# In a fused attention and mixture-of-experts kernel, the third expert's row gathers are tied behind the second expert's last low half

## The chip, the cores and the metric

The kernel runs on one core of one Trainium2 chip. The metric is device microseconds of one execution of the whole program. The kernel before took 590.61 us (median of three runs, 588.82 to 591.28). The profiled execution, from which all rows below come, took 590.45 us; its span, from the first profiled instruction to the last, is 588.60 us, so 1.85 us lie around the span.

The five engines are called as the profile calls them: PE (matmuls), DVE (VectorE), ACT (ScalarE), POOL (GpSimd) and SP (SyncE, which only issues DMAs here). Each engine runs its own queue of instructions strictly in order; semaphores tie the queues together.

## The reference

```
kv  = einsum('bhsd,bhse->bhde', k, v)            # 8 x 8 heads, 576 rows, 64 wide
out = einsum('bhsd,bhde->bhse', q, kv)
x   = out / sqrt(mean(out*out) + 1e-6) * g_norm  # then 4608 rows of 512
logits = x @ w_gate                              # 8 experts, the best one is taken
e = argmax(logits); gate = softmax(logits)[e]
h = relu(x[rows of e] @ w1[e])                   # 512 -> 1024
y = h @ w2[e]                                    # 1024 -> 512
out[row] = gate * y                              # at most 1152 rows per expert
```

## The kernel before

**Stages.** The first half of the program computes the attention, normalises and routes the rows, and writes each row (with its scale and its gate) to the DRAM table `x_dram`. The second half takes the eight experts in order of their row counts, r = 0 to 7, with fixed row budgets of 704, 672, 640, 624, 592, 576, 560 and 512. The expert r = 0 is begun early; "the second expert" is r = 1 (672 rows), "the third expert" is r = 2 (640 rows).

**An expert's matmuls.** Inputs and weights are split into a high and a low fp16 half, and three products stand for one fp32 product. The first layer makes eight blocks (j = 0 to 7) of hidden units: 24 matmuls (line 522) into a PSUM bank `hp`, of which there are two in turn; ACT then writes the high half `hh` (line 527) and DVE the low half `hl` (line 530), which frees the bank. The second layer (lines 568 and 577) multiplies by `w2`, ACT scales the result (`ysb`, line 593), and POOL scatters it to the output (line 598).

**An expert's rows.** While expert r is multiplied, `rows_beside(r + 1)` brings the rows of the next one, in tiles of 128 (r = 1: five full tiles and one of 32; r = 2: five). Each tile is gathered by an indirect DMA that POOL issues (`fetch`, line 433, into `xg`, four buffers), normalised into `xm` (line 441, two buffers; on DVE or POOL for r = 1, on POOL otherwise), its gate is copied (line 446, POOL), ACT rounds it to the high half (`pair`, line 465, two buffers), POOL subtracts for the low half (line 469), and SP issues a transposing DMA into `xs` (line 473). The first layer's products for all columns wait for these transposes.

**An expert's weights.** `weights(r + 1)` loads `raw` in eight pieces through SP (line 321), and DVE takes the largest magnitude of each eighth (`am`, line 337). Two tiny matmuls (lines 350 and 357) spread the maximum over the partitions, DVE works out a scale, ACT writes high halves (`w1h`, `w2h`, line 371), DVE low halves (`w1l`, `w2l`, line 377).

**What sets the order.** Every step is registered with `op(engine and planned duration, function, dependencies, key, ...)`, and `Plan.place()` plays the whole program through with the planned durations: an engine that is free takes, of the operations that are ready, the one with the smallest key. Instructions are emitted in the order found, so each engine's queue is fixed before the program runs. In `rows_beside` the gathers have the key of their expert's turn and everything behind them `key + 1`, so a ready gather of the third expert goes ahead of work of the same rank on POOL, and it is issued as soon as an `xg` buffer is planned to be free.

Of the kernel before, what the change touches and what calls it, by code (L numbers as in the profile page):

```python
# [78 lines left out]
class Ring:  # L79
# [3 lines left out]
    def new(self):  # L83
        self.holds.append(Hold(self.holds[-self.n] if len(self.holds) >= self.n else None))
        return self.holds[-1]
# [8 lines left out]
class Plan:  # L94
# [5 lines left out]
    def op(self, ways, fn, deps=(), key=0.0, takes=(), uses=(), late=0.0):  # L100

        ways = [ways] if isinstance(ways[0], str) else list(ways)
        o = Op(ways, fn, [d for d in deps if d is not None], list(takes), key, late)
        for h in takes + uses if isinstance(takes, tuple) and isinstance(uses, tuple) else list(takes) + list(uses):
            h.users.append(o)
        self.ops.append(o)
        return o
# [56 lines left out]
def attention_moe_kernel(  # L164
# [17 lines left out]
    P = 128  # L182
# [96 lines left out]
    first = cst.tile([P, E], F32, name="first")  # L279
# [130 lines left out]
    def spans(s0, s1):  # L410

        cuts = [s0] + list(range((s0 // P + 1) * P, s1, P)) + [s1]
        return [(a, b - a, NHI if a % P else a // P) for a, b in zip(cuts, cuts[1:])]
# [212 lines left out]
    def slots(pool, reg_ap, s0=0):  # L626

        c_reg = nc.vector.value_load(reg_ap, min_val=0, max_val=(E - 1) * NHI)
        both = []
        for tab_, nm in ((gidx_tab, "gi"), (sidx_tab, "si")):  # L630
            t = pool.tile([P, NHI + 1], I32, name=f"{nm}{s0}", bufs=3)
            nc.vector.tensor_copy(t[:, 0:NHI], tab_[:, ds(c_reg, NHI)])  # L632
            if s0 % P:
                nc.vector.tensor_copy(t[0:P - s0 % P, NHI:NHI + 1], t[s0 % P:P, s0 // P:s0 // P + 1])
            both.append(t)
        return both
# [27 lines left out]
    op = plan.op  # L664
# [411 lines left out]
    early = {}  # L1076
# [414 lines left out]
    op = plan.op  # L1491
# [59 lines left out]
    def rows_beside(r, key):  # L1551

        hold, sl, st = new("xs"), new("slots"), {}

        def cut(e):
            st["gi"], st["si"] = slots(mo, perm_i[0:1, 1, r:r + 1])

        cut_ = op(("V", 0.4), cut, [early["rank"]], key, (sl,))
        n = len(spans(0, BUDGET[r]))
        gates, turned, first, sent, asked = [], [], None, [], []  # L1560
        for i in range(n):
            xg, xm, pair = new("xg"), new("xm"), new("pair")

            def fetch(e, i=i):
                if i == 0:
                    st["x"] = Rows(mo, st["gi"], 0, BUDGET[r], BM, 4)
                st["x"].fetch(i)

            o = op(("P", 1.05), fetch, [cut_, first], key, (hold, xg), (sl,))
            first = first or o  # L1570
            asked.append(o)
            o = op(("D", GATHER), None, [o], key, (), (xg,))
            a = op([("V", 0.61), ("P", NORM)] if r == 1 else ("P", NORM),
                   lambda e, i=i: st["x"].norm(i, nc.vector if e == "V" else nc.gpsimd), [o], key - 5 if r == 1 else key + 1,
                   (xm,), (xg,))
            gates.append(op(("P", 0.25), lambda e, i=i: st["x"].gate(i, nc.gpsimd), [a], key + 1, (), (xg, hold)))
            a = op(("A", 0.52), lambda e, i=i: st["x"].pair_high(i), [a], key + 1, (pair,), (xm, hold))
            a = op(("P", PAIR), lambda e, i=i: st["x"].pair_low(i), [a], key + 1, (), (xm, pair, hold))
            a = op(("S", TURN), lambda e, i=i: st["x"].pair_turn(i), [a], key + 1, (), (pair, hold))
            sent.append(a)  # L1580
            turned.append(op(("D", TURNED), None, [a], key + 1, (), (pair, hold)))
        return st, hold, sl, gates, turned, sent, asked
# [50 lines left out]
    o = op(("S", 0.01), moved, [early["scaled"]], -9 * KEY, (), tuple(ews))  # L1633
# [6 lines left out]
    for r in range(E):  # L1640
        products(r, *args)
        key = KEY * r
        if r + 1 < E:
            before = [] if r > 1 else sent
            st, xs_hold, sl, gates, turned, sent, asked = rows_beside(r + 1, key + ROWS)
            sets, zs, w_holds = weights(r + 1, key + 1, before, asked[4:4 + 1] if r == 0 else [])
            args = (lambda st=st: st["x"], turned, turned, gates, xs_hold, lambda st=st: st["si"], sl, sets, zs, w_holds, 0,
                    BUDGET[r + 1])
        else:
            steps, o = plan_rest(), early["later"]  # L1650
            for _ in range(68):
                o = op(("V", 0.2), lambda e: next(steps, None), [o], key + 1)
# [36 lines left out]
```

## Time and profile before

| | |
|---|---|
| median of three runs | 590.61 us (588.82 to 591.28) |
| profiled execution | 590.45 us, span 588.60 us |
| PE busy | 535.5 us, 91% of the span |
| DVE, ACT, POOL busy | 381.2, 256.5, 222.5 us |
| mean granted PE clock | 0.976 of full speed |

PE is the engine that is busy longest. Of its idle time in the second half, the stretch of interest here is around 220 us from the span's start, where the matmuls of the second expert begin; those of the third begin at 287 us. Busy shares are read per stretch, since the stages have different limits, and a duration of POOL in the profile includes time in which the instruction was held up.

### The profile page before, as it was taken

How to read it: one execution, taken by the hardware profiler on the slowest of the kernel's cores; microseconds unless marked ns; L12 is line 12 of the kernel's file. 1: busy time of each engine (PE TensorE's matmuls, PEld its weight loads, DVE VectorE, ACT ScalarE, POOL GpSimd, SP SyncE). 2: the span in 40 equal slices, each digit the busy share in tenths (PEclk: the TensorE clock that was granted, in tenths of full speed). 3: DMA queues.
4: the chain of work that ended last, by engine and by line, in shares of the span. 5: the costliest groups of instructions: out<-in, count | busy, mean ns of one | idle time of the engine just before them, and what ended most of it. 6: DMA issues, size and time to landing. Idle time of an engine off the chain costs nothing.

```text
span 588.6 us, 11591 instructions
## 1 busy us (share of the span) xinstructions
PE 535.5 (91%) x4339; PEld 359.2 (61%) x4339; DVE 381.2 (65%) x999; ACT 256.5 (44%) x498; POOL 222.5 (38%) x299
## 2 busy tenths in 40 slices
PE   1888899878987997999999999999999999999995
PEld 1887798778533654654665467467648747845442
DVE  2376688889995877999998556719637634740200
ACT  1456476769621355382825151543525255211210
POOL 6002043355315677466541724364163452011011
PEclk9999799988999997999999999999999999999998
DMA  7999999957228768688861753646266332001001
GB/s 200 265 273 327 331 298 363 334 186 252 91 91 293 213 145 288 150 268 221 244 215 56 209 167 120 195 112 220 73 174 190 117 73 76 1 30 45 1 19 48
DMA packets 94302, 102.56 MB, mean 174 GB/s; under 512 B 51314, under 2 KB 75890, under 8 KB 93216
## 3 DMA queue, kind: packets, MB, share of 16 engines
q1 hardware_dynamic: 86240, 70.43, 44.2%
q0 software_dynamic: 8000, 31.32, 15.1%
q8 instruction: 36, 0.59, 0.4%
q14 instruction: 26, 0.21, 0.1%
HBM read 73.13 MB, written 20.61 MB: 159 GB/s over the span
## 4 chain that ended last, share of the span: by engine, by line
PE 38%; DVE 21%; issue 18%; DMA 11%; POOL 5%; ACT 3%; SPq 3%; POOLq 0%; DVEq 0%; ACTq 0%
PE hp L522 14%; PE yp L568 14%; DMA out_dram<-ysb,si 6%; DVE am L337 4%; DMA q_sb<-in_q_dram 4%; DVE w2l L377 4%; PE op L789 3%; DVE w1l L377 2%; PE yp L577 2%; PE qp L771 2%; DVE hl L530 2%; DVE ss L818 1%; SPq L686 1%; SPq L685 1%; PE a L707 1%
## 5 line engine op out<-in xcount | busy, mean ns | idle before, releaser
L522 PE MATMUL hp<-xs,w1h 128*128 128x320 f16 (+6 forms) x896 | 135.1, 302 | 5.9 <-DMA xs<-pair 4.3
L522 PEld LDWEIGHTS <-w1h 128*128 128x128 f16 x960 | 93.7, 99 | 47.4 <-issue 9.2
L598 POOL DMA_INDIRECT out_dram<-ysb,si x41 | 43.9, 1071 | 138.0 <-ACT ysb L593 103.2
L568 PEld LDWEIGHTS <-hh 128*128 128x128 f16 x560 | 54.3, 98 | 64.5 <-issue 1.9
L527 ACT ACTIVATE hh<-hp 128x320 f16<-128x320 f32 (+7 forms) x64 | 40.8, 638 | 116.1 <-PE hp L522 113.2
L337 DVE TENSOR_REDUCE am<-raw 128x1 f32<-128x512 f32 x120 | 75.6, 674 | 5.7 <-DMA raw<-in_moe_w_dram 5.5
L522 PE MATMUL hp<-xs,w1l 128*128 128x320 f16 (+6 forms) x448 | 71.6, 300 | 0.0
L530 DVE SCALAR_TENSOR_TENSOR hl<-hp,hh 128x320 f16<-128x320 f32 (+7 forms) x64 | 47.2, 737 | 36.0 <-ACT hh L527 35.8
L469 POOL TENSOR_TENSOR pair<-xm,pair 128x512 f16<-128x512 f32 (+5 forms) x35 | 42.6, 1222 | 73.2 <-ACT pair L465 73.1
L568 PE MATMUL yp<-w2h,hl 128*128 128x512 f16 x272 | 66.1, 386 | 0.0
L568 PE MATMUL yp<-w2h,hh 128*128 128x512 f16 x272 | 64.4, 379 | 0.8 <-ACT ysb L593 0.8
L568 PE MATMUL yp<-w2l,hh 128*128 128x512 f16 x272 | 64.4, 379 | 0.0
L789 PE MATMUL op<-kv_bd,qt 128*128 128x144 f32 (+1 forms) x384 | 58.5, 295 | 6.0 <-ACT qt L672 2.4
L593 ACT ACTIVATE ysb<-yp,ysc 128x512 f32<-128x512 f32 (+5 forms) x40 | 27.4, 684 | 83.2 <-PE yp L568 69.5
L522 PEld LDWEIGHTS <-w1l 128*128 128x128 f16 x480 | 46.7, 98 | 19.1
L433 POOL DMA_INDIRECT xg<-x_dram,gi x41 | 43.8, 1067 | 36.6 <-DVE gi L632 24.2
L789 PEld LDWEIGHTS op<-kv_bd,qt 128*128 128x128 f32 x384 | 50.7, 197 | 9.7 <-ACT o_sb L672 3.2
L377 DVE SCALAR_TENSOR_TENSOR w2l<-raw,sw,w2h 128x512 f16<-128x512 f32 x64 | 49.2, 815 | 9.7 <-ACT w2h L371 9.7
L377 DVE SCALAR_TENSOR_TENSOR w1l<-raw,sg,w1h 128x512 f16<-128x512 f32 x64 | 47.3, 788 | 0.9 <-ACT w1h L371 0.8
L568 PEld LDWEIGHTS <-hl 128*128 128x128 f16 x280 | 27.2, 99 | 33.5 <-issue 2.6
L371 ACT ACTIVATE w2h<-raw,sw 128x512 f16<-128x512 f32 x62 | 39.6, 711 | 5.9 <-PE yp L577 3.5
L371 ACT ACTIVATE w1h<-raw,sg 128x512 f16<-128x512 f32 x62 | 39.6, 711 | 4.8 <-DVE sg L366 3.8
(249 smaller groups left out, 666.3 us busy)
## 6 DMA issues: line engine op xcount, KB each, us to landing
raw<-in_moe_w_dram SPq DMA_DIRECT2D x64, 512.0 KB
x_dram<-o_sb POOLq DMA_DIRECT2D x8, 1152.0 KB
k_sb<-in_k_dram SPq DMA_DIRECT2D x16, 512.0 KB
v_sb<-in_v_dram SPq DMA_DIRECT2D x16, 512.0 KB
q_sb<-in_q_dram SPq DMA_DIRECT2D x16, 512.0 KB
x_dram<-o_sb POOLq DMA_DIRECT2D x8, 144.0 KB
k_sb<-in_k_dram SPq DMA_DIRECT2D x16, 64.0 KB
v_sb<-in_v_dram SPq DMA_DIRECT2D x16, 64.0 KB
```

Source lines behind the costliest of these rows:

```text
L337: nc.vector.tensor_reduce(out=am()[:, p:p + 1], in_=raw[:, sl(p)], axis=AX.X, op=ALU.max, apply_absolute_value=True)
L371: nc.scalar.activation(wh[:, sl(p)], raw[:, sl(p)], AF.Copy, scale=z["s"])
L377: nc.vector.scalar_tensor_tensor(out=wl[:, sl(p)], in0=raw[:, sl(p)], scalar=z["s"], in1=wh[:, sl(p)], op0=ALU.mult, op1=ALU.subtract)
L433: nc.gpsimd.indirect_dma_start(out=self.xg[i][0:n], out_offset=None, in_=x_dram[0:self.rows, :], in_offset=bass.IndirectOffsetOnAxis(ap=se ...
L469: nc.gpsimd.tensor_tensor(out=pair[0:n, 1], in0=self.xm[i][0:n], in1=pair[0:n, 0], op=ALU.subtract)
L522: nc.tensor.matmul(self.view(hp)[:, u], lhsT=w[:, c, j * P:(j + 1) * P], rhs=x[:, c, u * hw:(u + 1) * hw], start=(t == 0 and c == 0), stop ...
L527: nc.scalar.activation(self.out(self.hh, j), self.view(hp), AF.Relu)
L530: nc.vector.scalar_tensor_tensor(out=self.out(self.hl, j), in0=self.view(hp), scalar=0.0, in1=self.out(self.hh, j), op0=ALU.max, op1=ALU.s ...
L568: nc.tensor.matmul(yp[0:n, 0:DM], lhsT=h[:, j, o:o + n], rhs=w[:, j, :], start=(m == 0), stop=(m == len(self.terms) - 1))
L593: nc.scalar.activation(self.ysb[0:n], yp[0:n, 0:DM], AF.Copy, scale=self.ysc[0:n, i:i + 1])
L598: nc.gpsimd.indirect_dma_start(out=out[:, :], out_offset=bass.IndirectOffsetOnAxis(ap=self.sidx[0:n, col:col + 1], axis=0), in_=ysb[0:n], ...
L789: nc.tensor.matmul(ph.t[:, j * m:(j + 1) * m], lhsT=qt.t[:, i * P:(i + 1) * P], rhs=x, start=True, stop=True)
```

## The change

One dependency is added. For r = 1 each `pair_low` (line 469) is noted in `early["lows", 1]`; for r = 2 each gather depends, besides the slots and the expert's first gather, on the last of those. The list exists for r = 1 alone, so only the third expert's five gathers get the new dependency. No operation is added or taken away; the planner is run anew and may order all queues otherwise.

```diff
-            o = op(("P", 1.05), fetch, [cut_, first], key, (hold, xg), (sl,))
+            o = op(("P", 1.05), fetch, [cut_, first] + early.get(("lows", r - 1), [])[-1:], key, (hold, xg), (sl,))
...
             a = op(("P", PAIR), lambda e, i=i: st["x"].pair_low(i), [a], key + 1, (), (xm, pair, hold))
+            if r == 1:
+                early.setdefault(("lows", r), []).append(a)
```

POOL's queue in the kernel before, from the gates of the second expert's third and fourth tile to the scatter after its last low half. `gi_2751` are the row numbers of the third expert; `pair` of line 469 is a low half of the second:

```order
L446 COPY gt<-xg 128x1 x2
L433 DMA xg<-x_dram,gi_2751 128x576 x2
L469 TENSOR_TENSOR pair<-xm,pair 128x512 x2
L446 COPY gt<-xg 128x1
L433 DMA xg<-x_dram,gi_2751 128x576
L598 DMA out_dram<-ysb,si_2601 4608x512
L446 COPY gt<-xg 32x1
L433 DMA xg<-x_dram,gi_2751 128x576
L469 TENSOR_TENSOR pair<-xm,pair 128x512
L469 TENSOR_TENSOR pair<-xm,pair 32x512
L598 DMA out_dram<-ysb,si_2601 4608x512
```

The same stretch in the changed kernel:

```order
L446 COPY gt<-xg 128x1 x2
L469 TENSOR_TENSOR pair<-xm,pair 128x512
L441 TENSOR_TENSOR xm<-xg 128x512
L446 COPY gt<-xg 128x1
L469 TENSOR_TENSOR pair<-xm,pair 128x512
L598 DMA out_dram<-ysb,si_2601 4608x512
L469 TENSOR_TENSOR pair<-xm,pair 128x512
L446 COPY gt<-xg 32x1
L469 TENSOR_TENSOR pair<-xm,pair 32x512
L598 DMA out_dram<-ysb,si_2601 4608x512
L433 DMA xg<-x_dram,gi_2751 128x576 x3
```

Four gathers of the third expert have gone from between the low halves to behind them, and the normalisation of the second expert's fifth tile (line 441) has come over from DVE. One scatter (line 598) stays between the fourth and the fifth low half.

ACT's queue before, where the second expert's first layer begins:

```order
L593 ACTIVATE ysb<-yp,ysc 64x512
L371 ACTIVATE w2h_2648<-raw_2645,sw_3242 128x512 x8
L527 ACTIVATE hh<-hp 128x672
L465 CAST pair<-xm 128x512 x2
L527 ACTIVATE hh<-hp 128x672 x3
```

And in the changed kernel:

```order
L593 ACTIVATE ysb<-yp,ysc 64x512
L371 ACTIVATE w2h_2648<-raw_2645,sw_3246 128x512 x6
L527 ACTIVATE hh<-hp 128x672
L371 ACTIVATE w2h_2648<-raw_2645,sw_3246 128x512 x2
L465 CAST pair<-xm 128x512
L527 ACTIVATE hh<-hp 128x672
```

The first `hh` of the second expert stands behind six high halves of `w2` in place of eight. DVE's queue has the like: the first `hl` (line 530) came behind seven low halves of `w2` (line 377) and comes behind six.

## Rows read from the trace of the kernel before

**Rows 1.** What PE waited for, 200 to 300 us; columns in the first line.
```profile
engine line waited for: us in total, times, longest us
PE hp L522 <- DMA xs<-pair: 4.3, 1, 4.3
PE pt_max L357 <- DVE bm L354: 1.5, 2, 1.2
PE yp L588 <- DVE bmax L361: 1.2, 1, 1.2
PE hp L522 <- DVE p2t L302: 1.2, 1, 1.2
```

**Rows 2.** The same, 300 to 590 us.
```profile
PE hp L522 <- DVE hl L530: 0.4, 1, 0.4
```

**Rows 3.** Timeline of PE: start, duration, line, operation, tiles, count, [idle before it].
```profile
221.00 0.31 PE L522 MATMUL hp<-xs,w1h 128*128 128x336 f16 x1
225.65 4.16 PE L522 MATMUL hp<-xs,w1h 128*128 128x336 f16 x15 [4.34 <-DMA xs<-pair]
229.65 1.30 PE L522 MATMUL hp<-xs,w1l 128*128 128x336 f16 x8
230.79 2.44 PE L522 MATMUL hp<-xs,w1h 128*128 128x336 f16 x16
```

**Rows 4.** Stretches: length, busy per engine, granted PE clock, DMA share, GB/s.
```profile
219.00:222.00 3.00, 1.13 (x10) 0.75 (x7) 1.10 (x6) 0.74 (x2) 2.90 (x3) 1.00 0.46 150
222.00:225.00 3.00, 0.00 (x0) 0.00 (x0) 2.42 (x1) 3.00 (x6) 2.91 (x3) 0.61 1.00 199
225.00:229.00 4.00, 3.35 (x13) 1.79 (x14) 4.00 (x6) 1.83 (x3) 2.81 (x5) 0.50 0.77 265
```

**Rows 5.** SP's queue: the transpose of the second expert's last tile.
```profile
222.23 1.18 SPq L473 DMA_TRANSPOSE xs<-pair  x1
```

**Rows 6.** Timeline of POOL, 210 to 226 us.
```profile
210.47 1.52 POOL L469 TENSOR_TENSOR pair<-xm,pair 128x512 f16<-128x512 f32 x1 [2.42 <-ACT pair L465]
...
212.39 3.94 POOL L433 DMA_INDIRECT xg<-x_dram,gi  x1 [0.27 <-POOL gt L446]
216.64 1.51 POOL L598 DMA_INDIRECT out_dram<-ysb,si  x1 [0.31 <-DVE bm L354]
...
219.63 2.28 POOL L469 TENSOR_TENSOR pair<-xm,pair 128x512 f16<-128x512 f32 x2
222.08 1.02 POOL L598 DMA_INDIRECT out_dram<-ysb,si  x1 [0.17 <-ACT ysb L593]
223.12 2.10 POOL L441 TENSOR_TENSOR xm<-xg 128x512 f32<-128x512 f32 x2
```

**Rows 7.** Timeline of ACT, 211 to 232 us.
```profile
211.89 0.69 ACT L593 ACTIVATE ysb<-yp,ysc 128x512 f32<-128x512 f32 x1 [0.27 <-PE yp L568]
212.79 0.62 ACT L465 CAST pair<-xm 128x512 f16<-128x512 f32 x1 [0.21 <-DMA xs<-pair]
215.28 0.62 ACT L465 CAST pair<-xm 32x512 f16<-32x512 f32 x1 [1.87 <-DMA xs<-pair]
...
221.84 4.99 ACT L371 ACTIVATE w2h<-raw,sw 128x512 f16<-128x512 f32 x8
```

**Rows 8.** Timeline of DVE: two trains of weight lows, the first and last `hl`.
```profile
212.75 2.72 DVE L377 SCALAR_TENSOR_TENSOR w1l<-raw,sg,w1h 128x512 f16<-128x512 f32 x4
...
222.59 3.19 DVE L377 SCALAR_TENSOR_TENSOR w2l<-raw,sw,w2h 128x512 f16<-128x512 f32 x1 [1.35 <-ACT w2h L371]
...
231.75 0.86 DVE L530 SCALAR_TENSOR_TENSOR hl<-hp,hh 128x672 f16<-128x672 f32 x1 [2.01 <-ACT hh L527]
...
258.28 0.85 DVE L530 SCALAR_TENSOR_TENSOR hl<-hp,hh 128x672 f16<-128x672 f32 x1
```

**Rows 9.** Busy time again, in the second expert's layers (columns as in Rows 4).
```profile
240.00:260.00 20.00, 20.00 (x131) 12.55 (x130) 19.66 (x42) 11.58 (x19) 12.50 (x11) 1.00 0.63 160
```

**Rows 10.** The third expert's last transpose on SP and its first matmuls.
```profile
250.53 1.23 SPq L473 DMA_TRANSPOSE xs<-pair  x1
...
287.22 2.33 PE L522 MATMUL hp<-xs,w1h 128*128 128x320 f16 x16
```

## The prediction

> **What bounds the kernel now.** The waits of PE come first, since PE is the engine that is busy longest. Between 200 and 300 us one of them is 4.3 us: the first layer of the second expert waits for a transposed tile [rows 1]; behind 300 us PE waits for 0.4 us on any other engine's result [rows 2]. So whatever PE gains near 220 us should still be there at the end, unless a stretch before 300 us takes it back. PE's timeline shows the wait: one matmul at 221.00, ending at 221.31, the next at 225.65 [rows 3]. It also shows a second cost. Fifteen matmuls then take 4.00 us from start to start (229.65 less 225.65); eight take 1.14 us a little later (230.79 less 229.65), so fifteen should take 2.14, and 1.86 us are lost. The stretches say why: PE had done nothing from 221.3 on, and the granted clock, 1.00 up to 222, is 0.61 in the mean over the next 3 us and 0.50, the lower of its two levels (1.2 of 2.4 GHz), from 225 to 229 [rows 4].
>
> What PE waited for is the transpose of the sixth tile, which SP issued at 222.23 [rows 5]; from there to 225.65 are 3.42 us, a landing. It was issued late because POOL was late. POOL finished the fourth low half at 211.99. The casts for the fifth and sixth were done on ACT at 213.41 and 215.90 [rows 7], but these two low halves ran only from 219.63 to 221.91: between stand a gather for the third expert that took 3.94 us, a scatter of 1.51 and another gather [rows 6]. The 3.94 us are no work of POOL: DVE's train of four `w1l` ran from 212.75 to 215.47 [rows 8], and the gather came through 0.86 us behind it.
>
> **The change part by part.** Up to the fourth low half POOL gets one thing more, the fifth tile's normalisation, 1.05 us each by the pair of 2.10, and its gate; POOL was idle for 2.42 us before that low half [rows 6], so this costs nothing, and the xm buffer it needs is free when the third low half ends.
>
> From there, by the order of the changed queue: the scatter, the fifth low half, a gate, the sixth, a scatter, and only then gathers. The scatter's data are ready at 212.58 (211.89 and 0.69) [rows 7]. Its price has two ends. At the low end it takes 1.02 us, as the scatter at 222.08 [rows 6]: then the fifth low half can run from 213.6, the sixth behind its cast at 215.90, ending at about 217.1, the transpose goes out there and lands at 220.5. PE would not wait at all, and 4.34 us go. At the high end it fares as the gather at 212.39 did beside the same DVE train: done at 216.4. Then the fifth low half ends at 217.6 (1.14 each, half of 2.28), with the gate (some 0.2) the sixth at 218.9, and the transpose lands at 222.35. PE waits 1.04 us from 221.31, and 3.3 us go. I take the high end: it is the nearest row, the same place beside the same four instructions. The scatter could also be no help at all if the low halves are held again and again; that is the first rival.
>
> By the Trainium skill ("SBUF — State Buffer", section "Who interferes with whom"), a DVE instruction with two SBUF inputs holds up only POOL instructions that read SBUF; writing DMA descriptors needs the other, the write side, which the page marks as inferred. `w1l` has two SBUF inputs, so by that rule the scatter would not be held and the sum below would be 6.2 us, a time of 584.3. The gather of 3.94 us that ended just behind the train [rows 6, 8] speaks against the rule, so the row decides.
>
> The clock is the second term. Its bounds are 0 and the 1.86 us worked out above. In 219 to 222 PE was idle for 1.87 of 3.00 us and the clock was still 1.00 [rows 4]; it fell only in the next 3 us, in which PE did nothing. With matmuls from 222.35 on, little of that idle time is left, and I take the whole 1.86 us. But if the clock falls all the same, this term is nothing.
>
> The sum is 3.3 + 1.86 = 5.2 us. What the moved work hides behind: the five gathers start some 8 us to 16 us later than they did, and their rows are wanted at 287.22, while the last transpose of the third expert went out at 250.53 [rows 10]. Even with all the delay passed on, over 20 us are left. SP's queue has weight loads behind those transposes, and in the changed order one load of the fourth expert in front of the last; these have the same 30 us. Loads for the third expert stand behind the second expert's last transpose and so go out earlier by what it gains.
>
> What is late next is the chain through DVE. The first `hl` frees a bank for the third block of products. Before, it began at 231.75, released by ACT [rows 8]. Now the first block of 24 matmuls (three times 1.14) ends at 222.35 + 3.42 = 225.8; ACT has done six of the eight `w2h` (4.99 us for eight [rows 7]) by 225.6, its `hh` is done at 226.5, and DVE, six `w2l` behind 222.59 at 0.68 each (2.72 for four [rows 8]), is free at 226.7. If POOL's two normalisations hold the first `w2l` as they did before, when it took 3.19 us in place of 0.68 [rows 6, 8], it is 229.2. So `hl` ends at 227.5 to 230.0, and PE wants it at 222.35 + 6.84 = 229.2: up to 0.8 us of wait. From the first `hl` to the last DVE took 26.5 us (258.28 less 231.75) and was hardly ever idle (19.66 of 20.00 us [rows 9]). It starts 2.6 to 5.1 us earlier and has one low half of 0.68 us less to do on the way, so it is ready 3.3 to 5.8 us earlier, against 5.2 for PE. I cost this at nothing, with 1.9 us as the other end. The later waits of [rows 1], 1.5 us for the two tiny matmuls and 1.2 for a bank, are 2.7 us that an order shifted on DVE and PE may save or double; I take zero between 2.7 us gained and 2.7 us lost.
>
> So 590.45 - 5.2 = 585.25 us for the profiled execution, which lies 0.16 us under the median of 590.61; I say 585.3.
>
> **The rivals.** First, little comes of it (no change). The low halves are held by DVE's trains too (the one at 210.47 took 1.52 us, not 1.14 [rows 6]), PE starts at 224, 1.65 us earlier, its clock falls all the same, and DVE's chain sets the pace: 590.45 - 1.65 = 588.8. For it speaks that DVE is full from 240 to 260 [rows 9]; against it that the train which held POOL has ended at 215.47 and that DVE was idle for 2.01 us before the first `hl`, waiting for what PE now brings earlier [rows 8].
>
> Second, more comes of it. The scatter is not held (4.34 + 1.86 = 6.2), and the 2.7 us of later waits go as well, since the tiny matmuls and the `hl` of the third expert get other places: 8.9 us, 581.6. For it: each of these waits is on DVE, which has its chain earlier; against: PE comes earlier by as much.
>
> Third, slower. All ten POOL operations for the third expert's rows (five normalisations, five low halves) now fall between the first and last `hl` of the second, where before two of the normalisations lay ahead. One hold of the kind of 223.12 costs DVE 2.5 us (3.19 less 0.68 [rows 8]). It decides from the point at which DVE loses over 5.2 us more in that stretch than before: PE is only two banks ahead and then stands still with it. Four such holds more are 10.0 us: 590.45 - 5.2 + 10.0 = 595.3. Against: eight of the ten lay there before too, and DVE kept up.
>
> That the change doesn't do what it says, is ruled out by the order: all five gathers stand behind the last low half.
>
> **How the numbers follow.** The forecast (583 to 587.5) gets 0.54, the first rival 0.21 (587.5 to 592), the second 0.20 (580.5 to 583), the third 0.05. This kernel's measurement can tell about 0.5%, 2.95 us, from no change, so the border is 587.7 us: the forecast and the second rival lie under it, 0.75 with a little of either's edge; same is 0.20, slower 0.05. The range from 581.5 to 589.3 leaves out some of the second rival, part of the first, and the third, 0.2 together.
>
> **What would show it.** In the changed profile no gather of line 433 stands on POOL between the second expert's fourth and sixth low half; the last transpose of that expert goes out at 217 to 219 in place of 222.23; PE's wait for it is under 1.1 us; the granted clock stays at 1.00 from 221 to 229; the second layer and the third expert's first matmul (287.22) come about 5 us earlier, and everything behind keeps that. I am wrong if the transpose still goes out at 221 or later, if the clock falls although PE waits for a microsecond only, or if PE's new waits for `hl`, a bank or the tiny matmuls between 229 and 300 us are over 3 us in all.

## The result and the profile after

The changed kernel took 582.67 us (median of six runs, 578.99 to 586.47), the kernel before 590.16 us beside it (six runs, 588.50 to 591.40): a ratio of 0.9874 with a 95% interval of 0.9833 to 0.9916. The profiled execution took 582.53 us, its span is 580.73 us, 7.9 us shorter than before. Three later comparisons of the same two kernels, each on another of three chips, gave 0.9989, 0.9981 and 0.9916; what lies behind this spread is the main matter of the experiments.

The waits of PE from 200 to 300 us come first (total, times, longest), against [rows 1]:

```profile
PE pt_max L357 <- DVE bm L354: 2.5, 3, 1.2
PE pt_max L350 <- DVE a L347: 1.6, 1, 1.6
PE hp L522 <- DVE hl L530: 1.4, 2, 0.7
```

The wait for the transposed tile, 4.3 us, is gone. PE's timeline (start, duration, line, operation, count, [idle before it]) answers to [rows 3] and, in the last row, to [rows 10]:

```profile
217.39 0.60 PE L588 MATMUL yp<-ident,yt 128*64 128x128 f32 x4
217.82 2.46 PE L522 MATMUL hp<-xs,w1h 128*128 128x336 f16 x16
220.12 1.30 PE L522 MATMUL hp<-xs,w1l 128*128 128x336 f16 x8
221.26 2.44 PE L522 MATMUL hp<-xs,w1h 128*128 128x336 f16 x16
...
279.35 2.33 PE L522 MATMUL hp<-xs,w1h 128*128 128x320 f16 x16
```

The first product of the second expert runs through, 16 matmuls in 2.30 us from start to start, where before one ran alone and 15 took 4.00 us. The stretches (length, busy per engine, granted clock, DMA share, GB/s) show why, against [rows 4]:

```profile
216.00:219.00 3.00, 2.49 (x33) 1.86 (x30) 2.02 (x9) 0.93 (x2) 2.39 (x3) 1.00 0.49 133
219.00:222.00 3.00, 3.00 (x23) 2.06 (x22) 2.60 (x4) 3.00 (x6) 2.39 (x3) 1.00 0.92 317
222.00:225.00 3.00, 3.00 (x23) 2.06 (x22) 2.88 (x9) 2.27 (x4) 2.04 (x3) 1.00 1.03 398
```

PE is never idle for long, and the granted clock stays at 1.00. On POOL, SP and DVE, against [rows 6], [rows 5] and [rows 8]:

```profile
207.89 1.60 POOL L469 TENSOR_TENSOR pair<-xm,pair 128x512 f16<-128x512 f32 x1 [0.69 <-ACT pair L465]
210.28 1.07 POOL L598 DMA_INDIRECT out_dram<-ysb,si  x1 [0.79 <-ACT ysb L593]
211.38 1.16 POOL L469 TENSOR_TENSOR pair<-xm,pair 128x512 f16<-128x512 f32 x1
...
213.83 1.68 POOL L469 TENSOR_TENSOR pair<-xm,pair 32x512 f16<-32x512 f32 x1 [0.68 <-ACT pair L465]
215.67 1.28 POOL L598 DMA_INDIRECT out_dram<-ysb,si  x1 [0.17 <-issue]
217.25 1.00 POOL L433 DMA_INDIRECT xg<-x_dram,gi  x1 [0.30 <-issue]
```

```profile
215.53 1.18 SPq L473 DMA_TRANSPOSE xs<-pair  x1
```

```profile
205.73 4.31 DVE L377 SCALAR_TENSOR_TENSOR w1l<-raw,sg,w1h 128x512 f16<-128x512 f32 x4
...
213.10 3.62 DVE L377 SCALAR_TENSOR_TENSOR w1l<-raw,sg,w1h 128x512 f16<-128x512 f32 x4
...
223.39 0.85 DVE L530 SCALAR_TENSOR_TENSOR hl<-hp,hh 128x672 f16<-128x672 f32 x1
...
227.43 2.34 DVE L377 SCALAR_TENSOR_TENSOR w2l<-raw,sw,w2h 128x512 f16<-128x512 f32 x1
...
231.48 0.84 DVE L530 SCALAR_TENSOR_TENSOR hl<-hp,hh 128x672 f16<-128x672 f32 x1
...
253.11 10.26 DVE L377 SCALAR_TENSOR_TENSOR w2l<-raw,sw,w2h 128x512 f16<-128x512 f32 x8
```

The train of eight in the kernel before:

```profile
259.95 5.37 DVE L377 SCALAR_TENSOR_TENSOR w2l<-raw,sw,w2h 128x512 f16<-128x512 f32 x8
```

No gather stands between the low halves. The scatter at 210.28 falls between DVE's two `w1l` trains and is not held (1.07 us). The last transpose goes out at 215.53 in place of 222.23. Later on DVE one `w2l` takes 2.34 us, and a train of eight takes 10.26 us, where before it took 5.37: POOL's low halves and normalisations of the rows now lie beside them.

**Where 7.9 us came from.** Start-up varies between executions, so each stage is measured from the first of the first expert's matmuls of 320 columns ("mark"); up to there every queue has the same order in both kernels. "Transpose": SP issues the second expert's last transpose; "block 2": the second block of its first layer; "layer 2": its second layer; "third": the third expert's first matmul.

| execution | mark, us | transpose | block 2 | layer 2 | third | from there to the end |
|---|---|---|---|---|---|---|
| before | 192.09 | +30.14 | +38.70 | +63.78 | +95.14 | 301.42 |
| after | 189.15 | +26.38 | +32.10 | +57.84 | +90.19 | 301.38 |

Of 7.9 us, 2.94 lie ahead of the mark, 4.95 between it and the third expert, 0.04 behind. Only the 4.95 can be the change's, and not all of it need be: a second profile of the kernel before, below, has its third expert at +93.64 in place of +95.14.

### The profile page after: what moved, and what is told of

Same layout as the page of the kernel before. It is cut to its first block, busy times and chain, and to the rows that moved or that the text cites. A ratio compares the mean times of both kernels' runs of the same rounds, so it can differ in the third digit from the quotient of the medians.

```text
span 580.7 us, 11581 instructions
## 1 busy us (share of the span) xinstructions
PE 530.1 (91%) x4339; PEld 354.9 (61%) x4339; DVE 384.1 (66%) x998; ACT 256.0 (44%) x498; POOL 218.2 (38%) x300
## 4 chain that ended last, share of the span: by engine, by line
PE 28%; issue 19%; DMA 12%; DVE 11%; POOL 6%; ACT 2%; POOLq 0%; DVEq 0%; SPq 0%
PE hp L522 12%; PE yp L568 12%; DMA out_dram<-ysb,si 8%; DVE w2l L377 3%; DMA xg<-x_dram,gi 2%; DVE am L337 2%; POOL xg L433 2%; DVE hl L530 2%; PE yp L577 1%; POOL pair L469 1%; POOL xm L441 1%; PE op L522 1%; DMA raw<-in_moe_w_dram 1%; POOL out_dram L598 1%; DVE w1l L377 1%
## 5 line engine op out<-in xcount | busy, mean ns | idle before, releaser
L522 PE MATMUL hp<-xs,w1h 128*128 128x320 f16 (+6 forms) x896 | 133.5, 300 | 1.8 <-DVE hl L530 1.7
L598 POOL DMA_INDIRECT out_dram<-ysb,si x41 | 42.2, 1030 | 135.3 <-ACT ysb L593 104.1
L377 DVE SCALAR_TENSOR_TENSOR w2l<-raw,sw,w2h 128x512 f16<-128x512 f32 x64 | 53.2, 878 | 9.5 <-ACT w2h L371 9.5
L377 DVE SCALAR_TENSOR_TENSOR w1l<-raw,sg,w1h 128x512 f16<-128x512 f32 x64 | 52.3, 868 | 1.7 <-ACT w1h L371 1.7
```

The source lines that it names most:

```text
L377: nc.vector.scalar_tensor_tensor(out=wl[:, sl(p)], in0=raw[:, sl(p)], scalar=z["s"], in1=wh[:, sl(p)], op0=ALU.mult, op1=ALU.subtract)
L522: nc.tensor.matmul(self.view(hp)[:, u], lhsT=w[:, c, j * P:(j + 1) * P], rhs=x[:, c, u * hw:(u + 1) * hw], start=(t == 0 and c == 0), stop ...
L598: nc.gpsimd.indirect_dma_start(out=out[:, :], out_offset=bass.IndirectOffsetOnAxis(ap=self.sidx[0:n, col:col + 1], axis=0), in_=ysb[0:n], ...
```

## The experiments

Lines of a kernel with inserted code are shifted by 7 or 14. The last column of the table is explained under the third group.

| execution | mark | transpose | block 2 | layer 2 | third | to the end | PE's count late |
|---|---|---|---|---|---|---|---|
| before once more | 192.82 | +30.22 | +38.80 | +63.93 | +93.64 | 301.29 | 0.92 |
| after, second time | 186.39 | +26.02 | +38.22 | +62.79 | +95.14 | 301.99 | 5.12 |
| gathers moved only | 189.80 | +27.98 | +36.72 | +64.77 | +96.52 | 301.36 | 0.01 |
| PE kept busy | 187.80 | +30.11 | +36.97 | +61.95 | +92.40 | 302.16 | 0.92 |
| gathers behind scatter | 191.10 | +26.03 | +32.20 | +60.55 | +92.89 | 301.49 | 0.75 |
| gathers ahead of it | 188.66 | +26.03 | +39.10 | +64.93 | +97.28 | 301.97 | 5.09 |
| after, third time | 190.57 | +26.04 | +38.93 | +63.50 | +95.87 | 301.99 | 5.09 |
| behind, norms later | 191.78 | +26.03 | +32.20 | +62.75 | +94.21 | 304.35 | 0.76 |
| after, copy on ACT | 192.20 | +26.02 | +31.75 | +56.50 | +88.84 | 301.95 | 0.01 |
| before, copy on ACT | 190.28 | +30.16 | +38.32 | +63.44 | +93.28 | 300.68 | 0.01 |
| copy on ACT, hh ahead | 191.89 | +27.21 | +32.95 | +58.93 | +91.42 | 300.71 | 0.01 |
| after, fourth time | 193.87 | +27.01 | +32.73 | +57.59 | +90.14 | 301.42 | 0.01 |

### Is it the start, or the change?

**The kernel before, unchanged.**

> The kernel before, unchanged, once more with a profile. The change's profile is 7.9 us shorter: 2.9 us of it lie ahead of the first matmul of the first expert's rows (192.09 us before, 189.15 after), where no queue was changed, and 4.9 us between there and the third expert's first matmul (95.1 before, 90.2 after). Theory (the early 2.9 us are chance of an execution, from loads that arrive faster): the ratio is 1.000 within 0.3%; this profile's first matmul of the first expert lies somewhere from 189 to 193 us, and the stretch from there to the third expert's first matmul is again 95 us within 0.7. Rival (the changed program really starts faster): 192.1 us within 0.5 here, and 189.2 in every run of the changed kernel.

Measured: 589.12 us (12 runs), ratio 1.0004 (0.9978 to 1.0030), the wait for the tile 4.7 us. The third expert comes at +93.64, outside the 95 within 0.7 that was expected: of the 1.50 us against the first profile, 1.40 are two waits of PE for the tiny matmuls (0.23 at 273.53 and 1.17 at 283.63 there) that this execution doesn't have. **The changed kernel, unchanged**, on the same chip:

> The changed kernel, unchanged, once more. Theory: the stretch from the first to the third expert's first matmul is 90.2 us within 0.7, about 4.9 under before, and the time is 585.2 us, 5 us under before in the same call; the first matmul of the first expert lies from 189 to 193 us. Rival (the program really starts 2.9 us faster): it lies at 189.2 us and the time is 582.5, 7.5 to 8 under before.

Measured: 589.07 us (12 runs), ratio 0.9989 (0.9960 to 1.0018). The mark lies at 186.39 in this execution of the changed kernel and at 193.87 in another: it moves by over 7 us with nothing changed, so the 2.94 us of the first pair are no effect. But the 4.95 us are gone too, although the transpose went out as early as in the first. Columns as above:

```profile
213.85 0.38 PE L357 MATMUL pt_max<-bm,ones 1*128 1x1 f32 x2 [0.47 <-DVE bm L354]
219.09 1.03 PE L588 MATMUL yp<-ident,yt 128*64 128x128 f32 x4 [4.87 <-DVE bmax L361]
```

```profile
213.52 0.27 DVE L354 TENSOR_REDUCE bm<-pt_max 1x1 f32<-1x128 f32 x1
218.52 0.42 DVE L583 COPY yt<-yp 128x256 f32<-128x256 f32 x1 [4.73 <-remote]
218.86 0.15 DVE L361 COPY bmax<-pt_max 128x1 f32<-128x1 f32 x1
```

```profile
213.00:216.00 3.00, 0.76 (x16) 0.55 (x11) 0.79 (x2) 0.00 (x0) 2.39 (x3) 0.94 0.46 141
216.00:219.00 3.00, 0.00 (x0) 0.00 (x0) 0.48 (x2) 0.00 (x0) 1.34 (x2) 0.50 0.96 341
219.00:222.00 3.00, 2.91 (x12) 1.87 (x13) 1.08 (x6) 1.79 (x3) 0.83 (x1) 0.50 0.99 354
```

PE waits 4.87 us for the copy (`yt`, line 583) of the first expert's narrow tile, which it must turn (line 588) before the second expert begins. The clock falls to its lower level as it did in [rows 4]. A new wait, of nearly the size of the old one, has taken its place.

### The parts of the change

**The four gathers moved alone**, in the order of the kernel before:

```diff
+late = [at["fetch", 2, i] for i in range(4)]
+# put directly behind ("low", 1, 5), all else as before
```

> The order of the kernel before on every engine, but on GpSimd the third expert's first four gathers stand behind the second expert's last low half. Theory A (the gathers between the low halves are the whole cause): the last transpose of the second expert goes out some 4 us earlier against the first expert's first matmul (30.1 us behind it before), PE has no wait of over 1 us for a transposed tile, the clock stays at 1.00, and the stretch to the third expert is 90 to 91.5 us. Rival B (it is the other queues' new order, with hh and hl of the second expert ahead of two weight halves, that brings it): the stretch stays over 93 us. What the new order of the other queues is worth is the difference to 90.2.

Measured: 589.79 us (12 runs), ratio 1.0002 (0.9976 to 1.0028). POOL and DVE:

```profile
211.32 3.54 POOL L605 DMA_INDIRECT out_dram<-ysb,si  x1 [0.73 <-ACT ysb L600]
```

```profile
211.22 2.72 DVE L384 SCALAR_TENSOR_TENSOR w1l<-raw,sg,w1h 128x512 f16<-128x512 f32 x4
```

This is the high end of my first term: the scatter beside the four `w1l` takes 3.54 us, and the transpose goes out 2.16 us earlier (30.14 to 27.98), not 3.76. PE still waits 2.7 us, the clock falls for that as well (15 matmuls in 3.74 us from start to start), 2.6 us go to waits for `hl`, and the third expert comes at +96.52, on the rival's side of 93: nothing is left. In the changed kernel the train lies elsewhere on DVE and the scatter takes 1.07 us; that this new order gives the rest is read from these rows, and was not tried by itself.

**PE kept busy while it waits**, in the kernel before: 18 matmuls into a bank that nobody reads.

```diff
+idle = psx.tile([P, 512], F32, tag="x", name="idle")
+for _ in range(18):
+    nc.tensor.matmul(idle, lhsT=w[:, 0:P], rhs=w[:, 0:512], start=True, stop=True)
```

> The kernel before, with 18 more matmuls of 128x512 (0.216 us each, 3.9 us in all, into a spare bank that nobody reads) in front of the second expert's first product, so that PE works while it waits for the last transposed tile. It still cannot go on before that tile lands, 4.3 us after the first product was issued. Theory (the second term, the clock): the granted clock stays at 1.00 from 220 to 230 us, the first fifteen products take 2.1 us in place of 4.0, and the stretch from the first to the third expert is 1.9 us shorter than before, 93.3 us, if DVE keeps up. Rival (the products are slow for another reason, or DVE sets the pace there): the products stay slow, or they are fast and the stretch is still 95 us.

Measured: 587.60 us (12 runs), ratio 0.9981 (0.9951 to 1.0011), not to be told from 1. PE's timeline, and one stretch:

```profile
220.63 0.31 PE L522 MATMUL hp<-xs,w1h 128*128 128x336 f16 x1
221.50 2.30 PE L522 MATMUL hp<-xs,w1h 128*128 128x336 f16 x15 [0.56 <-DMA xs<-pair]
...
219.00:222.00 3.00, 2.44 (x14) 1.08 (x13) 3.00 (x2) 3.00 (x6) 1.96 (x3) 1.00 0.76 222
```

With work put into the wait the clock stays at 1.00, and the 15 matmuls take 2.14 us from start to start (the next row begins at 223.64), not 4.00: 1.86 us, as worked out ahead. Block 2 comes 1.73 us earlier and the third expert 2.74 and 1.24 us earlier than in the two profiles of the kernel before.

### What makes the copy late

Three kernels on a third chip. The changed order, with its first three gathers **behind the scatter of the narrow tile** instead of ahead of it:

```diff
+late = [at["fetch", 2, i] for i in range(3)]
+# put directly behind the first expert's last write
```

> The changed kernel, but the three gathers that follow the second expert's last low half stand behind the next scatter too. That scatter waits for the first expert's narrow tile, so for DVE's copy of it (line 583), and the gathers can no longer run beside this copy. In the last profile of the changed kernel the copy's matmuls were done at 213.38 us and the copy ran only at 218.52, behind three gathers in a row (214.13 to 217.65); in the first profile it ran 0.34 us behind its matmuls, with the same gathers 0.4 us behind it. Theory (the gathers hold the copy in those executions in which they come first, and that took the gain back): the copy runs within 0.6 us of its matmuls, PE waits under 1 us for it, the stretch from the first to the third expert's first matmul is 90.2 us within 0.7 (95.1 where the copy was held), and the time is 4 to 5 us under before, 584.5 to 585.5. Rival (the change is worth nothing on this chip for another reason): the stretch stays over 93 us, the time is as before.

Measured: 588.03 us (12 runs), ratio 0.9971 (0.9941 to 1.0001). The same three **ahead of the scatter before that**, directly behind the last low half:

> The changed kernel, but the three gathers stand ahead of the scatter that now parts them from the second expert's last low half, so that they run always when the copy of line 583 becomes ready. Theory: the copy waits in every execution until some 0.4 to 0.9 us behind the third gather, 3 us or more behind its matmuls, PE waits 3 to 4 us there, its clock falls as before, and the stretch is 93.5 to 95 us. Rival (gathers don't hold the copy): the copy runs within 0.6 us of its matmuls and the stretch is 90.2 us.

Measured: 592.90 us (12 runs), ratio 1.0070 (1.0040 to 1.0101), slower. And **the changed kernel a third time**:

> The changed kernel, unchanged, a third time, beside the two above. Theory: the order of copy and gathers is decided in each execution by less than half a microsecond. Where the copy comes first the stretch is 90.2 us, where the gathers come first it is 95.1, nothing lies between, and the median time lies between that of the kernel with the gathers behind the copy and that of before. Rival: the stretch takes other values.

Measured: 588.31 us (12 runs), ratio 0.9981 (0.9945 to 1.0016). The wait at line 588 is 0.5, 4.8 and 4.8 us in the three: on this chip the gathers' place decides it. The first of them, expected at +90.2 at the third expert, comes at +92.89 all the same. In the kernel with the gathers ahead POOL and DVE read:

```profile
214.81 1.26 POOL L440 DMA_INDIRECT xg<-x_dram,gi  x1 [0.16 <-issue]
216.38 0.95 POOL L440 DMA_INDIRECT xg<-x_dram,gi  x1 [0.30 <-issue]
217.63 0.95 POOL L440 DMA_INDIRECT xg<-x_dram,gi  x1 [0.30 <-issue]
218.88 1.02 POOL L605 DMA_INDIRECT out_dram<-ysb,si  x1 [0.30 <-issue]
```

```profile
215.79 0.27 DVE L361 TENSOR_REDUCE bm<-pt_max 1x1 f32<-1x128 f32 x1
220.76 0.42 DVE L590 COPY yt<-yp 128x256 f32<-128x256 f32 x1 [4.70 <-remote]
```

The copy comes 0.85 us behind the last of four indirect DMAs in a row. I first took this for DVE held by POOL, and that was the theory of the last group. What the copy waits for tells otherwise: it waits for PE's count of finished work, and the trace's record of that count rises just ahead of it. The count's lateness against the end of the matmuls, which is modelled, is the table's last column. With the indirect DMAs that POOL issued in a row from there on:

| execution | DMAs in a row | end of the last | PE's count rises |
|---|---|---|---|
| before (first profile) | 1 gather | 219.62 | 219.97 |
| gathers behind scatter | 1 scatter | 218.54 | 218.85 |
| after, second time | scatter, 3 gathers | 217.65 | 218.50 |
| gathers ahead | 3 gathers, scatter | 219.91 | 220.74 |
| after, third time | scatter, 3 gathers | 221.87 | 222.67 |
| gathers moved only | none | | 217.55, at once |

In the first five of these PE's count comes only when POOL has got through its DMAs, 0.3 to 0.4 us behind a single one and 0.8 to 0.9 us behind four. A DMA under way is not enough for that: in the first profile of the kernel before, the counts of lines 568 and 350 came 0.01 us behind their ends (216.17 and 216.28), with the gather of 3.94 us running to 216.3 [rows 6]. The count of the tiny matmul of line 357 rises 0.04 us behind it in the second profile (218.54), though PE began that one at 213.85: the two matmuls were reported together, and whether they ran late or were only told late, the trace does not say.

**The gathers behind the scatter, and the fourth expert's norms later**, to take away what the first of the three gave back:

```diff
+[o] + (early["writes", 1][1:2] if r == 3 else [])
```

> As the kernel with the gathers behind the copy, and the fourth expert's rows are normalised only behind the second expert's second scatter (GpSimd's order alone follows from it). In the first profile of the changed kernel DVE's eight low halves of the third expert's w2 took 10.26 us (253.11 to 263.37) in place of 5.30, since three of them were held beside GpSimd's normalisations and low halves, and PE then waited 1.6, 1.2 and 0.8 us for DVE. Theory (these waits are what the change gave back): the eight take under 7 us, PE's waits for DVE between 250 and 285 us fall from 3.6 to under 1.5 us, and the stretch is 87 to 89 us. Rival (they are held elsewhere as much): 90 us.

Measured: 589.25 us (12 runs), ratio 0.9989 (0.9962 to 1.0016). This fell: the one wait for `hl` was 2.9 us, the clock fell behind it (16 matmuls in 4.44 us from start to start), and the turned tile of the third expert's turn cost 3.2 us more. The loss in the kernel with the gathers behind the scatter shows on ACT and PE of its own profile:

```profile
230.31 0.62 ACT L472 CAST pair<-xm 128x512 f16<-128x512 f32 x1 [3.98 <-POOL xm L448]
230.83 0.72 ACT L534 ACTIVATE hh<-hp 128x672 f16<-128x672 f32 x1
```

```profile
232.50 1.73 PE L529 MATMUL hp<-xs,w1h 128*128 128x336 f16 x11 [2.20 <-DVE hl L537]
```

The third expert's cast stands ahead of the second expert's `hh` in ACT's queue. The later the gathers, the longer it waits, and PE with it.

### The copy on another engine

**The changed kernel with the narrow tile's copy on ACT** (first expert only):

```diff
-nc.vector.tensor_copy(self.yt[:, 0:KD * n], yp[:, 0:KD * n])
+(nc.scalar.copy if e == "A" else nc.vector.tensor_copy)(self.yt[:, 0:KD * n], yp[:, 0:KD * n])
```

> The changed kernel, in which the first expert's narrow tile (yt, line 583) is copied out of PSUM by ACT instead of DVE. Theory A (DVE's copy is held as long as POOL issues one gather behind the other): ACT's copy starts within 0.5 us of the end of its matmuls, PE's wait of 4.8 us for the turned narrow tile is gone (under 0.7 us), the third expert's first matmul comes +89.5 to +91 us behind the first of the first expert's beside rows, as in the first profile of the changed kernel (+90.2), not +95 to +96; time 0.990 to 0.994 of the kernel before. Rival B (what holds the copy is not DVE, but PSUM or the tile's buffer, or the landing of a DMA): ACT's copy is late by 5 us too, +95, time 0.997 to 1.000. Rival C (the wait is gone, but the gain is lost behind it): +90, and the time is within 0.3% of the changed kernel's run beside it.

Measured: 584.72 us (7 runs), ratio 0.9911 (0.9873 to 0.9949). **The kernel before with the same edit**:

> The kernel before, with the same copy on ACT: what the copy alone is worth. Theory A: PE waits there for the sixth transposed tile in any case, so nothing comes of it: wait for the tile 4 to 4.7 us, third expert's first matmul at +93.5 to +95.5, time 0.998 to 1.002 of the kernel before. Rival (DVE's late copy was a cost of the kernel before too): 0.9 us less, 0.997 or lower.

Measured: 588.64 us (12 runs), ratio 1.0004 (0.9977 to 1.0031). **The changed kernel with it, and the second and third `hh` put ahead of the two casts**:

```diff
+for i in (0, 1):
+    cast, hh = at["high", 2, i], at["hh", 1, i + 1]
+    # hh, and what it needs, is put ahead of cast
```

> The changed kernel with the copy on ACT, and on ACT the second expert's second and third hh each ahead of the third expert's first and second cast, which stood in front of them and waited for a normalisation on POOL. Theory A with its second part (those casts are what the bank waits of the first profile came from): as the run with the copy alone, and PE's waits for hl between 225 and 245 us, 0.7 and 0.7 us there, are under 0.3 us together; third expert's first matmul at +88.5 to +90, time 0.988 to 0.992 of the kernel before. Rival: the waits for hl come from DVE's own trains, and stay within 0.3 us of the run with the copy alone.

Measured: 583.34 us (7 runs), ratio 0.9899 (0.9863 to 0.9935), the fastest of the four, but its interval holds the ratios of the other two changed kernels. **The changed kernel a fourth time**:

> The changed kernel once more, beside the three others on one chip. Theory A: either the narrow tile's copy starts ahead of the gathers (PE's wait there under 0.7 us, +90) or behind them (4.8 us, +95 to +96); in twelve timed runs both occur, median 0.995 to 0.999 of the kernel before, and slower than the run with the copy on ACT by 2 to 5 us. Rival: the first comparison (0.987) comes again.

Measured: 584.57 us (12 runs), ratio 0.9916 (0.9886 to 0.9945).

On this chip nothing was late, in any of the four, and so the first does not test what it was made for. With the copy on ACT:

```profile
218.80 0.40 PE L577 MATMUL yp<-hh,w2l 128*128 128x64 f16 x8
219.66 0.38 PE L357 MATMUL pt_max<-bm,ones 1*128 1x1 f32 x2 [0.46 <-DVE bm L354]
219.97 0.63 PE L588 MATMUL yp<-ident,yt 128*64 128x128 f32 x4
```

```profile
219.23 0.37 ACT L583 COPY yt<-yp 128x256 f32<-128x256 f32 x1 [2.21 <-PE yp L577]
```

But the changed kernel as it was, beside it, has the copy on DVE, with the same scatter under way and PE's count at once (221.87, 0.01 behind 221.85), and it is as fast:

```profile
221.02 1.28 POOL L598 DMA_INDIRECT out_dram<-ysb,si  x1 [0.17 <-issue]
222.19 0.40 DVE L583 COPY yt<-yp 128x256 f32<-128x256 f32 x1
```

The theory that DVE's copy is held is not borne out: where it was late, PE's count was late, and where PE's count was not, DVE's copy was not either. Even the order of the kernel before, with a gather running (216.82 to 217.81), has the count at once here (217.28), where in all three other profiles of that order it was 0.9 us late.

The theory that the casts cost the changed kernel its own waits for `hl` fell as well. With `hh` ahead of them PE still waited 0.94 us for `hl` at 236.21, where the run with the copy alone has no such wait before 293.57. It comes from DVE:

```profile
230.66 2.94 DVE L391 SCALAR_TENSOR_TENSOR w2l<-raw,sw,w2h 128x512 f16<-128x512 f32 x1
233.53 1.86 DVE L351 TENSOR_REDUCE am<-raw 128x1 f32<-128x512 f32 x3
235.31 0.84 DVE L544 SCALAR_TENSOR_TENSOR hl<-hp,hh 128x672 f16<-128x672 f32 x1
```

```profile
230.87 1.17 POOL L483 TENSOR_TENSOR pair<-xm,pair 128x512 f16<-128x512 f32 x1
231.99 1.06 POOL L455 TENSOR_TENSOR xm<-xg 128x512 f32<-128x512 f32 x1
```

One `w2l` beside a low half and a normalisation of the third expert takes 2.94 us in place of 0.73; in the first profile after it took 2.34.

**What stays open.** Why PE's count waits for POOL's DMAs in eight profiles (seven on two chips, and the first before), and not in five with a DMA under way just the same (four on one chip, and the first after). The order alone is not the cause, since the changed kernel's is the same in its four profiles. Nor is it a matter of this place alone. In the five profiles in which it comes at once (the prompt kind) no count of PE in the whole execution comes over 0.2 us behind its modelled end; in each of the nine others, that of the gathers moved alone among them, 7 to 15 seem to. Those nine also have two to seven records of the count fewer than the pattern of the five, so some of these late counts are only gaps in the trace, and a part of the recording itself in the delay is not ruled out. That it is the chip is likely and not shown; whether ACT's copy would help where the count is late was not tried.

What fits is the size: the comparisons with a profile of the prompt kind gave 0.9874 and 0.9916, those with the late kind 0.9989 and 0.9981. The two profiles of the first comparison are of different kinds, before late and after prompt. In the prompt profiles the third expert comes at +93.28 before and at +88.84 after, both with the copy on ACT, and at +90.19 and +90.14 in the changed kernel as it was: a gain of 3.1 to 4.4 us. In the late ones it comes at +95.14 and +93.64 before and at +95.14 and +95.87 after: no gain.

## Why the prediction came out

- **The time**: 585.3 was forecast for an execution that took 582.53. Of the 2.7 us between, 2.94 are the start-up of these two executions, 192.09 against 189.15. From the mark on, 5.2 were forecast and 4.95 (with 0.04) measured. Some of this is luck: against the second profile of the kernel before it is 3.45, and two of the three later comparisons, at 589.07 and 588.31 us, lie outside the forecast's 583 to 587.5.
- **The transposed tile** (3.3 us forecast): the step that failed is "I take the high end". The scatter was not held (1.07 us), since the DVE train beside which I placed it had ended by 210.04 and the next began at 213.10. The whole wait went, 4.3 us: the low end, which stood in the sum's range. Where DVE's train stays in its old place the scatter's high end comes true, 3.54 us, though the transpose then gains 2.16 us and not the 3.3 of the sum. The 3.94 us of [rows 6] were rightly put down to the train, against the Trainium skill's rule ("SBUF — State Buffer", section "Who interferes with whom"); the 3.54 us agree with the row again, and not with the rule.
- **The clock** (1.86 us): right, in the first profile and, by itself, with PE kept busy. It hangs on there being no long wait at all, of whatever origin.
- **DVE's chain and the later waits** (0, with 1.9 and 2.7 lost as the other ends): mis-sized, and here the step that failed is "I cost this at nothing". My own sign of being wrong, over 3 us of PE's waits for `hl`, a bank or the tiny matmuls between 229 and 300 us, came: they are 5.0 us (0.69 and 0.72 for `hl`, 1.61, 1.17 and 0.84 for the tiny matmuls; 3.9 without the 1.17, which stood there before too), against 2.9 before. Up to block 2 the change gains 6.60 us (38.70 less 32.10): 4.34 for the tile, 1.86 for the clock, and 0.7 as the wait of 1.18 ahead of the turned tile becomes one of 0.46 for `bm`, less 0.35 by which the first expert's tail ended later. By the third expert 1.65 of it are given back: PE's waits on that stretch were 1.7 us before (the tiny matmuls, 0.23, 0.30 and 1.17) and are 3.5 now (0.69 for `hl`, then 1.61 and 1.17 for the tiny matmuls). Against the second profile of the kernel before, with 0.3 us of such waits, 3.25 are given back. The 1.61 stand behind DVE's train of 10.26 us, the 0.69 behind the `w2l` of 2.34.
- **So the sum was right by misses that cancel, which is luck**: a gain 1.0 us too small for the tile (and 0.4 more ahead of block 2), and a loss of 1.65 us, or 3.25, set at nothing for what is late next.
- **What I did not see**: the first expert's narrow tile. Its copy was 0.92 us late behind a gather in the profile before already (matmuls' end 219.08, copy 220.00), hidden by the wait for the transposed tile, and I cost the moved gathers only by what waits for their rows, not by what stands beside them. With three gathers in a row at that place PE waited 4.8 us and lost the clock in two profiles of four, all that the change gains. In those the first rival's time comes true, "little comes of it", by another mechanism.
- **The third rival**, DVE's holds, was real: DVE lost 1.7 us in the one `w2l` and 4.9 in the train of eight, and PE, which is some banks ahead, 2.3 us of it.

## What to carry over

A wait that is taken away uncovers what it hid: look in the old profile for everything that was late beside it, on the same path, even where it cost nothing there. When a train of indirect DMAs is moved, cost it by its new neighbours as well as by its consumers. And compare one kernel with itself before a gain of 1% is put down to an edit: this one gave 0.987 to 0.999 by chip and execution.

## What the runs showed of the hardware

- PE's count of finished matmuls came up to 5.1 us behind their modelled end, until 0.8 us behind the last of four indirect DMAs that POOL issued in a row, in some executions of a kernel and not in others; the cause is open. The profile names such a wait "remote" or names the instruction behind it.
- The start of the program, to the same matmul, took from 186.39 to 193.87 us in four profiles of one kernel.
- POOL's low half and normalisation stretched one DVE instruction with two SBUF inputs from 0.73 to 2.94 us, and four such DVE instructions stretched a scatter from 1.07 to 3.54 us.
